# Block attention and a gated MLP on one core: the diagonal blocks of a pair's two heads transposed together

## The chip, the cores and the metric

The kernel runs on one core of a Trainium2 chip. The metric is the device time of one execution in microseconds. Before the change it is 771.0 us, the median of three runs (768.85, 771.0 and 771.5 us).

## What is computed

Eight batches of 576 rows. First an attention of 8 heads with 64 columns each, in which a row sees the keys of its own 64-row block and of all blocks before it; the heads' outputs stand side by side as 512 columns. Then a gated MLP whose gate mixes rows.

```python
scores = (1.0 / np.sqrt(D)) * np.matmul(q, k.transpose(0, 1, 3, 2))     # 8 x 8 x 576 x 576
scores = np.where(block_i >= block_j, scores, -1e9)                      # blocks of 64
attn = np.exp(scores - scores.max(-1, keepdims=True))
attn = attn / (attn.sum(-1, keepdims=True) + 1e-09)
x = heads_side_by_side(np.matmul(attn, v))                               # 8 x 576 x 512
h = gelu_tanh(x @ w_in)                                                  # 1024 columns
u, v = h[..., :512], h[..., 512:]
v_s = np.einsum('ts,bsd->btd', w_sg, layernorm(v) * g_ln) + b_sg[None, :, None]
return x + (u * v_s) @ w_out
```

## The kernel before

**Pairs.** Attention goes by pairs of heads, 32 in all, four to a batch. The two heads (a = 0, 1) lie on partitions 0 to 63 and 64 to 127 of the loaded q and k. `Scores` (L315) computes a pair's scores in float32 precision from split halves, for five query tiles i = 0 to 4 of 64, 128, 128, 128 and 128 rows. Tile i sees `EXT[i]` = 64 + 128 i keys, so its last 64 keys are its diagonal block: only its lower 64 rows see them (for i = 0, all of its 64). `maximum` (L349) takes the scores out of PSUM on VectorE (DVE) into `prob[a][i]`, with mask and running maximum; `exponent` (L364) makes probabilities of them in place on ScalarE (ACT), with their sums. Tile 4 has more keys than a PSUM bank has room for, so `FIRST` (L388) cuts it in two halves of 288 keys, put together with tiles 1 and 0.

**Values.** `Values` (L405) multiplies by v. TensorE (PE) needs the keys on partitions, so `turn` (L415) transposes 128x128 blocks of `prob` through PSUM banks pA, pB and pC, and a copy by ACT or DVE (`TE`, L398) takes each bank to a tile pt. `PLACES` (L399) says which block lands where: per head four blocks in A, five in B, five in C. The diagonal tile of i has only 64 keys; it is filled up with zeros to 128 (the zero fill is done once, L162 to L172) and transposed whole, of which 64 columns are used. `turn_sums` (L436) transposes tile 0 of each head, and the inverse sums spread over 64 columns (`rx`, five transposes), into banks pd and pe; ACT copies them to `rb`. `products` (L462) then runs 30 products, v as weights (128 keys by 64 columns), heads alternating, into bank ob and a corner of pe; `normalise` (L477) multiplies by the inverse sums and stores the tile to DRAM (`spill`).

**Loads.** All DMAs are issued in order from SyncE's queue (SP). `load_v` (L126) loads v of a pair as one DMA of 128 x 4 x 128 and one of 64 x 128 into one of two buffers; `load_qk` (L104) loads q and k two pairs ahead, GpSimd (POOL) splits them.

**The MLP as filler.** When a batch's four pairs are done, its MLP is cut into chunks (`v_part`, `u_part`, `s_part`, `o_part`). `slot` (L760), used for pairs 4 to 31, puts chunks (`hole`) between a pair's transposes, the next pair's scores and the products. `opening_slot` (L721), used for pairs 0 to 3, has no chunks to put there; meanwhile the weights of the MLP are loaded and split by ACT, DVE and POOL (`load_weight`, L212), until pair 8. PE's instructions stay in the order in which the code is written. Those of DVE, ACT and POOL do so for pairs 0 to 3; later a scheduler orders them, as it does the queue of SP throughout.

Of the kernel before, what the change touches and what calls it, by code (L numbers as in the profile page):

```python
# [9 lines left out]
F32 = mybir.dt.float32  # L10
# [10 lines left out]
def kernel(  # L21
# [12 lines left out]
    nc = tc.nc  # L34
# [54 lines left out]
    def turn(out, in_):  # L89
        return tensor.transpose(out, in_, ident)  # L90
# [34 lines left out]

    def load_v(n):  # L126
        b, h = PAIRS[n]
        v_f = v_bufs[n % 2]
        cols = slice(h * D, (h + 2) * D)
        nc.sync.dma_start(  # L130
            v_f[:, : NT - 1, :],
            v[b, : (NT - 1) * P, cols].rearrange("(j p) d -> p j d", p=P),
        )
        nc.sync.dma_start(v_f[:TAIL, NT - 1, :], v[b, S - TAIL :, cols])
        vals[n] = v_f

    load_qk(0)


    ident = cp.tile([P, P], F32, name="ident")  # L140
    make_identity(nc, ident)
    def warm(t, k):
        for _ in range(k):
# [12 lines left out]


    for s in (0, 1):
        t = cp.tile([P, NT, 2 * D], F32, name=f"v_f{s}")
        gpsimd.memset(t[TAIL:, NT - 1, :], 0.0)  # L160
        v_bufs.append(t)
    prob = []  # L162
    for s in (0, 1):
        row = []
        for i in range(NT):
            t = cp.tile([P, P * (i + 1)], F32, name=f"prob{s}_{i}")
            if i:
                gpsimd.memset(t[:, EXT[i] :], 0.0)
            else:
                gpsimd.memset(t, 0.0)  # L170
            row.append(t)
        prob.append(row)  # L172


    wi_h = cp.tile([P, NC, DFF], F32R, name="wi_h")
# [139 lines left out]
    class Scores:  # L315
# [33 lines left out]
        def maximum(self, a, i, lo, hi):  # L349

            r, e = slice(0, QN[i]), EXT[i]
            m = self.negm[a][r, i : i + 1]
            behind["V"] = vector.tensor_tensor_reduce(
                prob[a][i][r, lo:hi],
                self.where[a, i, lo],
                mask[r, MW - (hi - lo) :] if 0 < i and hi == e else mask[r, : hi - lo],
                -0.125,
                3.0e38 if lo == 0 else m,
                op0=ALU.add,
                op1=ALU.min,  # L360
                accum_out=m,
            )
# [36 lines left out]
    PLACES = {  # L399
# [3 lines left out]
    }  # L403

    class Values:  # L405
# [6 lines left out]
            self.sm = sc.sm  # L412
            self.pt = {}

        def turn(self, a, which):  # L415

            t = bank("p" + which)
            for i, j, c in PLACES[which]:
                turn(t[:, c : c + P], prob[a][i][:, P * j : P * (j + 1)])
            pt = sp.tile([P, 512], F32, tag="pt", name="pt" + which, bufs=6)  # L420
            copy(TE[a, which], pt, t)
            for i, j, c in PLACES[which]:
                self.pt[a, i, j] = pt[:, c + BLK : c + P] if i == j else pt[:, c : c + P]

        def inverse(self):

# [8 lines left out]

        def turn_sums(self):  # L436

            def spread(i):
                return self.rx[:, i, :]
# [4 lines left out]
            for i in (0, 1, 2):  # L444
                c = 2 * BLK + (i and BLK + P * (i - 1))
                turn(t[:, c : c + P], spread(i))
            for i in (3, 4):
                turn(t2[:, P * (i - 3) : P * (i - 2)], spread(i))
            w = 2 * BLK + EXT[2]
            d = sp.tile([P, 2 * BLK + S], F32, tag="rb", name="rb", bufs=1)  # L450
            copy("a", d[:, :w], t[:, :w])
            copy("a", d[:, w:], t2[:, : 2 * P])
            for a in (0, 1):
                self.pt[a, 0, 0] = d[:, a * BLK : (a + 1) * BLK]
            self.rb = d[:, 2 * BLK :]
            self.o0 = t2[:, 2 * P : 2 * P + BLK]

        def products(self):

            self.ob = bank("ob")  # L460
            for i in (4, 3, 2, 1, 0):
                for j in range(i + 1):  # L462
                    c = BLK if i == j and i else 0
                    w = BLK if i == j else P
                    c += P * (i - 1)
                    for a in (0, 1):
                        r = slice(a * D, (a + 1) * D)
                        dst = self.ob[r, c : c + w] if i else self.o0[r, :]
                        mm(
                            dst,  # L470
                            self.v[:, j, r],
                            self.pt[a, i, j],
                            start=j == 0,
                            stop=j == i,
                        )

        def normalise(self):  # L477

# [51 lines left out]
    def v_part(b, vv, vn, vn_t, u, g_s):  # L530
        need("v")
        x_s = xs[b]
        for st in range(NT):
            rows = P if st < NT - 1 else TAIL
            ss = slice(st * P, (st + 1) * P)
            acc = accumulator("accv")
            terms = []
            for c in range(NC):
                hi, lo, both = x_s[c]
                if st < NT - 1:  # L540
                    terms += [(hi[:, ss], wi_h, c), (lo[:, ss], wi_h, c), (hi[:, ss], wi_l, c)]
                else:
                    terms += [(both, wi_h, c), (both, wi_l, c)]
            for y, (l, w, c) in enumerate(terms):
                mm(acc, l, w[:, c, DH:], start=(y == 0), stop=(y == len(terms) - 1))
            x = vv[st] = page(F32, DH, "vv")[:rows, :]
            if st < NT - 1:
                last = scalar.copy(x, acc).ins
            else:
                vt = sp.tile([P, DH], F32, tag="pt", name="vt", bufs=6)  # L550
# [169 lines left out]

    def opening_slot(n, va):  # L721

        va.turn(0, "A")
        va.turn(1, "A")
        va.turn(0, "B")
        va.turn(1, "B")
        va.inverse()
        split_pending()
        va.turn(0, "C")
        va.turn(1, "C")  # L730
        load_v(n + 1)
        load_qk(n + 2)
        nx = Scores(n + 1)
# [26 lines left out]
    def slot(n, va):  # L760
# [4 lines left out]
            load_v(n + 1)  # L765
        if n + 2 < N:
            load_qk(n + 2)
        va.turn(0, "A")
        va.turn(1, "A")
        hole(g[0])  # L770
        run_side(k)
        split_pending()
        load_share(n, 0)
        va.turn(0, "B")
        va.turn(1, "B")
        hole(g[1])
        run_side(k)
        va.turn(0, "C")
        va.turn(1, "C")
        va.turn_sums()  # L780
        hole(g[2])
        run_gelu()
# [94 lines left out]
```

## Time and profile before

| | |
|---|---|
| median of three runs | 771.0 us |
| the profiled execution | 770.48 us, of which 768.7 us are the span of the profile |
| DVE, ACT, POOL busy | 483.5, 438.3, 299.2 us |
| mean granted TensorE clock | 0.993 of full speed |
| DMA | 65.84 MB, 86 GB/s on average; queue q1 takes 27.0% of the sixteen engines' span |

The profile is of one execution. An engine's busy time is the union of its instructions' records. PE means matmuls and transposes, PEld the loads of their stationary operand, which run beside them. A matmul's record overlaps the next one's, so the number of them in a stretch of time tells more than the length of one. Almost every row carries line 60, because all engine calls pass through one helper there: groups are told apart by their tiles. A row reads out<-in, and in a row of a timeline the bracket at its end is the idle time before it and what ended that. In the profile, a transpose of a block of `prob` is a matmul with `prob` as weights and the identity streaming through.

### The profile page before, as it was taken

The numbers are of one execution on the slowest core, as the hardware profiler recorded it, in microseconds if no ns is written. First come the engines' busy times: TensorE is split into PE (matmuls) and PEld (weight loads), VectorE is DVE, ScalarE is ACT, GpSimd is POOL, SyncE is SP. The second block draws the span as 40 slices with busy tenths as digits, with TensorE's granted clock in tenths as the row PEclk, the third lists the DMA queues.
The fourth block names the chain that finished last, engine by engine and source line by source line (L and its number), as shares of the span: only waits on it lengthen the run. The fifth ranks groups of instructions, "written<-read, shape, count | busy, mean of one in ns | idle before, by whom it ended". The sixth has DMA issues, their size and how long they took to land.

```text
span 768.7 us, 18262 instructions
## 1 busy us (share of the span) xinstructions
PE 751.7 (98%) x7106; PEld 711.2 (93%) x7106; DVE 483.5 (63%) x1477; ACT 438.3 (57%) x1096; POOL 299.2 (39%) x382
## 2 busy tenths in 40 slices
PE   8779998999999999999999999999999999999998
PEld 8778997989999899999999899998999989998998
DVE  6898789775945468544776348663495644942632
ACT  6666868558734767337754377544874467731600
POOL 3666695544234333243434234341234522322121
PEclk9989999999999999999999999999999999999999
DMA  8235233224232213312242112511124211120032
GB/s 261 82 103 178 64 107 92 77 90 133 85 119 62 63 64 109 94 47 63 64 140 78 33 61 76 172 48 48 49 91 141 63 42 53 53 88 17 1 124 93
DMA packets 46922, 65.84 MB, mean 86 GB/s; under 512 B 4082, under 2 KB 22514, under 8 KB 46836
## 3 DMA queue, kind: packets, MB, share of 16 engines
q1 hardware_dynamic: 46836, 64.67, 27.0%
q8 instruction: 56, 0.92, 0.5%
q14 instruction: 30, 0.25, 0.1%
HBM read 45.78 MB, written 18.87 MB: 84 GB/s over the span
## 4 chain that ended last, share of the span: by engine, by line
PE 92%; DVE 6%; ACT 1%; issue 1%; DMA 0%; POOL 0%; SPq 0%; DVEq 0%; ACTq 0%; POOLq 0%
PE accs L60 15%; PE accv L60 14%; PE acco L60 13%; PE accu L60 12%; PE s L60 10%; PE ob L60 10%; PE pB L60 5%; PE pC L60 5%; PE pA L60 3%; PE pd L60 2%; DVE w L60 2%; DVE prob L60 2%; PE pe L60 1%; ACT prob L60 1%; DVE vv L566 1%
## 5 line engine op out<-in xcount | busy, mean ns | idle before, releaser
L60 ACT ACTIVATE prob<-prob,negm 128x576 f32<-128x576 f32 (+3 forms) x320 | 176.4, 553 | 72.2 <-DVE negm L60 69.4
L60 DVE CUSTOM_DVE_ANT_0 prob<-s,mask 128x288 f32<-128x288 f32 (+3 forms) x320 | 121.5, 424 | 47.7 <-PE s L60 47.0
L60 POOL TENSOR_TENSOR xh<-x,xh 128x64 fp32r<-128x64 f32 x32 | 10.4, 325 | 205.5 <-DVE xh L60 145.4
L60 POOL TENSOR_TENSOR gl<-u,gh 128x288 fp32r<-128x288 f32 x64 | 51.8, 813 | 95.7 <-DVE gh L60 95.5
L60 PE MATMUL accu<-xh,wi_h 128*128 128x288 f32 x256 | 78.4, 306 | 0.0
L60 PE MATMUL accs<-ws_h,vh 128*128 128x288 f32 x256 | 77.9, 304 | 0.0
L60 PE MATMUL acco<-gh,wo_h 128*128 128x288 f32 x256 | 77.6, 303 | 0.0
L60 PE MATMUL accs<-ws_h,vl 128*128 128x288 f32 x256 | 75.6, 295 | 1.3 <-DVE vl L60 1.3
L60 PE MATMUL acco<-gl,wo_h 128*128 128x288 f32 x256 | 75.5, 295 | 0.0
L60 PE MATMUL accu<-xl,wi_h 128*128 128x288 f32 x256 | 75.5, 295 | 0.0
L60 PE MATMUL accs<-ws_l,vh 128*128 128x288 f32 x256 | 75.5, 295 | 0.0
L60 PE MATMUL accu<-xh,wi_l 128*128 128x288 f32 x256 | 75.4, 295 | 0.0
L60 PE MATMUL acco<-gh,wo_l 128*128 128x288 f32 x256 | 75.3, 294 | 0.0
L60 PE MATMUL accv<-wi_h,xh 128*128 128x512 f32 x160 | 65.3, 408 | 0.0
L60 DVE TENSOR_TENSOR u<-accs,u 128x288 f32<-128x288 f32 x64 | 29.1, 455 | 54.4 <-PE accs L60 53.9
L60 PE MATMUL accv<-wi_l,xh 128*128 128x512 f32 x160 | 63.0, 393 | 0.0
L60 PE MATMUL s<-kh,qh 64*128 64x288 f32 (+4 forms) x384 | 62.6, 322 | 0.0
L60 ACT ACTIVATION_READ_ACCUMULATOR prob<-prob,negm 128x1 f32 x320 | 59.9, 187 | 0.0
L60 PE MATMUL s<-kh,ql 64*128 64x288 f32 (+4 forms) x384 | 58.4, 301 | 0.0
L60 PE MATMUL s<-kl,qh 64*128 64x288 f32 (+4 forms) x384 | 57.3, 299 | 0.0
L60 ACT COPY vv<-accv 128x512 f32<-128x512 f32 x32 | 18.6, 581 | 67.1 <-PE accv L60 67.1
L60 PE MATMUL pB<-ident,prob 128*128 128x128 f32 x320 | 43.6, 283 | 8.5 <-DVE negm L60 6.8
(113 smaller groups left out, 2108.5 us busy)
## 6 DMA issues: line engine op xcount, KB each, us to landing
q_f<-in_qT SPq DMA_DIRECT2D x32, 288.0 KB, 3.6
k_f<-in_kT SPq DMA_DIRECT2D x32, 288.0 KB, 2.8
spill<-x SPq DMA_DIRECT2D x32, 288.0 KB, 2.9
xr<-spill SPq DMA_DIRECT2D x32, 288.0 KB, 2.9
out_T<-xr SPq DMA_DIRECT2D x32, 288.0 KB, 2.1
v_f<-in_v SPq DMA_DIRECT2D x32, 256.0 KB, 3.2
w<-in_w_in SPq DMA_DIRECT2D x16, 256.0 KB, 4.8
xr<-in_w_out SPq DMA_DIRECT2D x8, 256.0 KB, 2.7
```

Of the source, the lines that this page charges most:

```text
L60: return lambda *a, **k: pin(method(*a, **k), self.letter)
L566: tc.keep_in_program_order(nc.vector.scalar_tensor_tensor(x, x, stats[:rows, st, 0:1], g_bc[:rows, :], op0=ALU.subtract, op1=ALU.mult))
```

## The change

Both heads' probabilities of a query tile now lie in one tile of 2 x `EXT[i]` columns. The second head's keys stand there in falling order of their 64-key blocks, so that its diagonal block comes first and lies beside the first head's, which is last: columns 128 i to 128 i + 128 hold both. One transpose turns the two, with keys of head 0 on partitions 0 to 63 and of head 1 on 64 to 127. For i > 0 the lower 64 rows are wanted, so these go through a shifted identity (`turned`), which puts them first; the next transpose overwrites the other half. The five go to pd with the first two of the spread sums; the other three sums go to pe.

The remaining blocks off the diagonal are 20 for a pair, in five banks A0, A1, B0, B1 and C. DVE writes the second head's scores block by block in falling order, and tile 4 is cut at key 256, a whole number of blocks. The values follow: `v_f` has the halves of each 128-key group swapped for head 1, and a second tile `v_d` holds the diagonal blocks' values, head 0 on the upper and head 1 on the lower 64 partitions, with zeros beside them; so a diagonal product of one head still runs over 128 partitions. v now comes in seven DMAs with rows of 64 columns (256 bytes) where there were two with rows of 128 (512 bytes), and the diagonal blocks are read twice.

```diff
@@ load_v @@
+        v_f, v_d = vals[n] = v_bufs[n % 2]
+        lo, hi = slice(0, BLK), slice(BLK, P)
+        for a, r in ((0, lo), (1, hi)):
+            cols = slice((h + a) * D, (h + a + 1) * D)
+            x = v[b, : (NT - 1) * P, cols].rearrange("(j p) d -> p j d", p=P)
+            if a == 0:
+                nc.sync.dma_start(v_f[:, :, r], x)
+            else:
+                nc.sync.dma_start(v_f[lo, :, r], x[hi])
+                nc.sync.dma_start(v_f[hi, :, r], x[lo])
+            nc.sync.dma_start(v_d[r, : NT - 1, r], x[lo])
+            nc.sync.dma_start(v_d[r, NT - 1, r], v[b, S - TAIL :, cols])
@@ setup @@
+    turned = cp.tile([P, P + BLK], F32, name="ident")
+    ident = turned[:, :P]
+    gpsimd.tensor_copy(turned[:, P:], turned[:, :BLK])
+        t = cp.tile([P, NT - 1, 2 * D], F32, name=f"v_f{s}")
+        d = cp.tile([P, NT, 2 * D], F32, name=f"v_d{s}")
+    pairs = [cp.tile([P, 2 * EXT[i]], F32, name=f"prob{i}") for i in range(NT)]
+    prob = [[pairs[i][:, a * EXT[i] : (a + 1) * EXT[i]] for i in range(NT)] for a in (0, 1)]
@@ Scores @@
+            out = blocks(prob[a][i][r, :])
+            out = out[:, ::-1, :][:, lo // BLK : hi // BLK, :] if a else out[:, lo // BLK : hi // BLK, :]
-        FIRST = ((4, 0, SH), (1, 0, EXT[1])), ((4, SH, S), (0, 0, EXT[0]))
+        HALF = 256
+        FIRST = ((4, 0, HALF), (1, 0, EXT[1])), ((4, HALF, S), (0, 0, EXT[0]))
@@ Values @@
-    TE = {(0, "A"): "a", (1, "A"): "v", (0, "B"): "a", (1, "B"): "v", (0, "C"): "v", (1, "C"): "a"}
+    TE = {"A0": "a", "A1": "v", "B0": "a", "B1": "v", "C": "v"}
     PLACES = {
...
+        "A0": [(0, 4, j) for j in range(4)],
+        "A1": [(1, 4, j) for j in range(4)],
+        "B0": [(0, 3, 0), (0, 3, 1), (0, 3, 2), (0, 1, 0)],
+        "B1": [(1, 3, 0), (1, 3, 1), (1, 3, 2), (1, 1, 0)],
+        "C": [(0, 2, 0), (0, 2, 1), (1, 2, 0), (1, 2, 1)],
     }
@@ turn_sums @@
-            for a in (0, 1):
-                turn(t[:, a * BLK : a * BLK + P], prob[a][0])
+            for i in range(NT):
+                c = slice(i * BLK, i * BLK + P)
+                first = turned[:, BLK:] if i else ident
+                tensor.transpose(t[:, c], pairs[i][:, P * i : P * (i + 1)], first)
...
-            copy("a", d[:, :w], t[:, :w])
-            copy("a", d[:, w:], t2[:, : 2 * P])
+            copy("a", d[:, :512], t)
+            copy("a", d[:, 512:], t2[:, : 3 * P])
+            self.dg = [d[:, i * BLK : (i + 1) * BLK] for i in range(NT)]
@@ products @@
+                        if j < i:
+                            x, y = v_f[:, j, r], self.pt[a, i, j]
+                            dst = self.ob[r, P * (i - 1) : P * i]
+                        else:
+                            x, y = v_d[:, i, r], self.dg[i]
```

The tiles pt have five buffers where they had six, as a pair fills five. In what follows a name's number tells tiles apart: `prob_113` is the new tile of i = 3 for both heads, `prob_4_113` was head 0's of i = 4.

On PE, the first pair's transposes stood in this order before (pA, pB and pC, then after the next pair's scores pd and pe):

```order
L60 MATMUL pB<-ident,prob_4_113 128x128
L60 MATMUL pB<-ident,prob_3_111 128x128 x4
L60 MATMUL pB<-ident,prob_4_123 128x128
L60 MATMUL pB<-ident,prob_3_121 128x128 x4
L60 MATMUL pC<-ident,prob_1_107 128x128 x2
L60 MATMUL pC<-ident,prob_2_109 128x128 x3
L60 MATMUL pC<-ident,prob_1_117 128x128 x2
L60 MATMUL pC<-ident,prob_2_119 128x128 x3
```

and stand in this order now:

```order
L60 MATMUL pB_252<-ident,prob_113 128x128 x3
L60 MATMUL pB_252<-ident,prob_111 128x128
L60 MATMUL pB_259<-ident,prob_113 128x128 x3
L60 MATMUL pB_259<-ident,prob_111 128x128
L60 MATMUL pC<-ident,prob_112 128x128 x4
```

The diagonal blocks of i = 1 to 4 are gone from pB and pC; those of i = 1 moved ahead, from pC to pB, as far as they are off the diagonal. They come back in turn_sums, in this piece of PE's difference, which follows the scores of the next pair:

```order
-L60 MATMUL pd<-ident,prob_0_105 128x128
-L60 MATMUL pd<-ident,prob_0_115 128x128
-L60 MATMUL pd<-ident,rx 128x128 x3
-L60 MATMUL pe<-ident,rx 128x128 x2
+L60 MATMUL pd<-ident,prob_110 128x128
+L60 MATMUL pd<-ident,prob_111 128x128
+L60 MATMUL pd<-ident,prob_112 128x128
+L60 MATMUL pd<-ident,prob_113 128x128
+L60 MATMUL pd<-ident,prob_114 128x128
+L60 MATMUL pd<-ident,rx 128x128 x2
+L60 MATMUL pe<-ident,rx 128x128 x3
```

On DVE, the first maxima of the second pair (negm is the negated maximum, read out by a row of its own) stood like this before; a bracket names the engines whose semaphores an instruction waits for:

```order
L60 COPY ptC<-pC 128x512 [waits PE_49]
L60 ISA prob_4_113,negm<-s,mask 128x288 [waits PE_49]
L60 ISA negm 128x1
L60 ISA prob_1_107,negm<-s,mask 128x192
L60 ISA negm 128x1
L60 ISA prob_4_123,negm<-s,mask 128x288 [waits PE_49]
L60 ISA negm 128x1
L60 ISA prob_1_117,negm<-s,mask 128x192
L60 ISA negm 128x1
L60 ISA prob_4_113,negm<-s,mask,negm 128x288 [waits DVE_49,PE_49]
```

and now:

```order
L60 COPY ptC<-pC 128x512 [waits PE_49]
L60 ISA prob_114,negm<-s,mask 128x256 [waits PE_49]
L60 ISA negm 128x1
L60 ISA prob_111,negm<-s,mask 128x192 [waits PE_49]
L60 ISA negm 128x1
L60 ISA prob_114,negm<-s,mask 128x4x64
L60 ISA negm 128x1
L60 ISA prob_111,negm<-s,mask 128x3x64
L60 ISA negm 128x1
L60 ISA prob_114,negm<-s,mask,negm 128x320 [waits DVE_49,PE_49]
```

The maximum of tile 1 has a wait of its own now: it overwrites columns that the second transpose of pd reads. The second head's maxima are written in blocks of 64 (4x64, 3x64).

On SP's queue, the third time that a buffer of v is filled anew, before (spill is the normalised tile on its way to DRAM):

```order
L134 DMA v_f_101<-in_v 64x128 [waits DMAHW7_49,PE_49]
L130 DMA v_f_101<-in_v 128x4x128 [waits PE_49]
L108 DMA q_f<-in_qT 128x576 [waits DMAHW4_49,DMAHW1_49,Pool_49]
L483 DMA spill<-x 128x576 [waits DMAHW2_49,DVE_49]
L109 DMA k_f<-in_kT 128x576 [waits DMAHW6_49,DMAHW3_49,Pool_49]
```

and now:

```order
L139 DMA v_d_103<-in_v 64x64 [waits DMAHW3_49,PE_49]
L139 DMA v_d_103<-in_v 64x64 [waits DMAHW4_49,PE_49]
L134 DMA v_f_102<-in_v 128x4x64 [waits DMAHW5_49,PE_49]
L138 DMA v_d_103<-in_v 64x4x64 [waits DMAHW6_49,PE_49]
L136 DMA v_f_102<-in_v 64x4x64 [waits DMAHW7_49]
L490 DMA spill<-x 128x576 [waits DMAHW0_49,DVE_49]
L137 DMA v_f_102<-in_v 64x4x64 [waits DMAHW1_49]
L138 DMA v_d_103<-in_v 64x4x64 [waits DMAHW2_49,PE_49]
L108 DMA q_f<-in_qT 128x576 [waits DMAHW3_49,Pool_49]
L109 DMA k_f<-in_kT 128x576 [waits DMAHW4_49,Pool_49]
```

v's pieces stand on both sides of the spill, and the load of q, which stood ahead of the spill, follows them all.

More of the change, by code (lines that the diff above doesn't have):

```diff
@@ L158 @@
     for s in (0, 1):
[L159 to L172, printed above, removed]
+        t = cp.tile([P, NT - 1, 2 * D], F32, name=f"v_f{s}")
+        d = cp.tile([P, NT, 2 * D], F32, name=f"v_d{s}")
+        for a in (0, 1):
+            r = slice(a * D, (a + 1) * D)
+            gpsimd.memset(d[r, :, (1 - a) * D : (2 - a) * D], 0.0)
+        v_bufs.append((t, d))
+    pairs = [cp.tile([P, 2 * EXT[i]], F32, name=f"prob{i}") for i in range(NT)]
+    prob = [[pairs[i][:, a * EXT[i] : (a + 1) * EXT[i]] for i in range(NT)] for a in (0, 1)]
+    gpsimd.memset(pairs[0][BLK:, :], 0.0)
     wi_h = cp.tile([P, NC, DFF], F32R, name="wi_h")
@@ L352, in maximum, with blocks @@
             m = self.negm[a][r, i : i + 1]
+            def blocks(x):
+                return x.rearrange("p (n c) -> p n c", c=BLK)
+            out = blocks(prob[a][i][r, :])
+            out = out[:, ::-1, :][:, lo // BLK : hi // BLK, :] if a else out[:, lo // BLK : hi // BLK, :]
             behind["V"] = vector.tensor_tensor_reduce(
-                prob[a][i][r, lo:hi],
-                self.where[a, i, lo],
-                mask[r, MW - (hi - lo) :] if 0 < i and hi == e else mask[r, : hi - lo],
+                out,
+                blocks(self.where[a, i, lo]),
+                blocks(mask[r, MW - (hi - lo) :] if 0 < i and hi == e else mask[r, : hi - lo]),
                 -0.125,
@@ L413, in __init__, with turn @@
             self.pt = {}
-        def turn(self, a, which):
+        def turn(self, which):
             t = bank("p" + which)
[L418 to L423, printed above, removed]
+            pt = sp.tile([P, 512], F32, tag="pt", name="pt" + which, bufs=5)
+            for c, (a, i, j) in enumerate(PLACES[which]):
+                c = slice(c * P, (c + 1) * P)
+                k = BLK + P * (i - 1 - j) if a else P * j
+                turn(t[:, c], prob[a][i][:, k : k + P])
+                self.pt[a, i, j] = pt[:, c]
+            copy(TE[which], pt, t)
         def inverse(self):
@@ new lines, in turn_sums @@
+            for i in (0, 1):
+                turn(t[:, W + i * BLK : W + i * BLK + P], self.rx[:, i, :])
+            for i in (2, 3, 4):
+                turn(t2[:, P * (i - 2) : P * (i - 1)], self.rx[:, i, :])
+            d = sp.tile([P, W + S], F32, tag="rb", name="rb", bufs=1)
+            copy("a", d[:, :512], t)
+            copy("a", d[:, 512:], t2[:, : 3 * P])
+            self.dg = [d[:, i * BLK : (i + 1) * BLK] for i in range(NT)]
+            self.rb = d[:, W:]
+            self.o0 = t2[:, 3 * P : 3 * P + BLK]
@@ L458, in products @@
         def products(self):
             self.ob = bank("ob")
+            v_f, v_d = self.v
             for i in (4, 3, 2, 1, 0):
                 for j in range(i + 1):
-                    c = BLK if i == j and i else 0
-                    w = BLK if i == j else P
-                    c += P * (i - 1)
                     for a in (0, 1):
                         r = slice(a * D, (a + 1) * D)
[L468 to L475, printed above, removed]
+                        if j < i:
[3 more added lines that the diff above has]
+                            x, y = v_d[:, i, r], self.dg[i]
+                            c = P * (i - 1) + BLK
+                            dst = self.ob[r, c : c + BLK] if i else self.o0[r, :]
+                        mm(dst, x, y, start=j == 0, stop=j == i)
@@ L767, in slot @@
             load_qk(n + 2)
-        va.turn(0, "A")
-        va.turn(1, "A")
+        va.turn("A0")
+        va.turn("A1")
         hole(g[0])
```

43 lines of the change are left out of this document (10 added, 33 removed), and 3 rows, old and new, of the table PLACES.

## The prediction

> **What bounds the kernel now.** I read the busy shares first, then PE's waits, then stages of the span.
>
> ```profile
> PE 751.7 (98%) x7106; PEld 711.2 (93%) x7106; DVE 483.5 (63%) x1477; ACT 438.3 (57%) x1096; POOL 299.2 (39%) x382
> PE 92%; DVE 6%; ACT 1%; issue 1%; DMA 0%; POOL 0%; SPq 0%; DVEq 0%; ACTq 0%; POOLq 0%
> ```
>
> PE is busy for 98% of the span, and the chain that ended last is PE's own work for 92% of it. Busy matmuls overlap in the records, so the next question is whether PE ever stands still. These are rows of PE's waits (engine, tile, whom it waited for: us in total, times, longest), and of busy time by stage (each engine's busy us, then the granted clock, the DMA share and GB/s).
>
> ```profile
> PE pB L60 <- DVE negm L60: 6.8, 3, 3.5
> PE pA L60 <- ACT vh L60: 1.8, 1, 1.8
> PE accs L60 <- DVE vl L60: 1.3, 1, 1.3
> 40.00:55.00 15.00, 12.31 (x133) 11.02 (x133) 13.58 (x43) 10.12 (x31) 9.43 (x13) 0.88 0.29 85
> 90.00:110.00 20.00, 20.00 (x213) 19.50 (x212) 16.17 (x50) 16.70 (x42) 19.66 (x25) 1.00 0.38 110
> 110.00:150.00 40.00, 36.84 (x387) 35.30 (x386) 35.70 (x95) 26.50 (x65) 23.54 (x27) 1.00 0.25 79
> 300.00:400.00 100.00, 100.00 (x960) 95.06 (x957) 59.97 (x195) 59.59 (x151) 37.42 (x45) 1.00 0.27 84
> ```
>
> There are three stages. In the opening (pairs 0 to 3) DVE is busy for 13.58 of 15 us and PE waits for it. While the weights are split (up to 150 us) PE waits twice, 1.8 and 1.3 us. After that PE never waits before its last matmul, at full clock: from 300 to 400 us it has 100.00 of 100 us, with DVE and ACT at 60%. In this last stage a matmul less is its time less, as long as nothing new becomes late.
>
> **The price of one transpose.** Weight loads run ahead of their matmuls at the same pace; one full pair shows that pace without overlap (start, us, engine, operation, count).
>
> ```profile
> 384.75 1.14 PEld L60 LDWEIGHTS pC<-ident,prob 128*128 128x128 f32 x10
> 385.86 0.25 PEld L60 LDWEIGHTS pd<-ident,prob 128*128 128x128 f32 x2
> 386.08 0.36 PEld L60 LDWEIGHTS pd<-ident,rx 128*128 128x128 f32 x3
> 386.41 0.25 PEld L60 LDWEIGHTS pe<-ident,rx 128*128 128x128 f32 x2
> 386.63 0.19 PEld L60 LDWEIGHTS acco<-gh,wo_h 128*128 128x128 f32 x1
> ```
>
> Ten take 385.86 - 384.75 = 1.11 us, the next seven 386.63 - 385.86 = 0.77 us: **0.111 us each**, not the 283 ns that one matmul's record lasts.
>
> **What goes.** The groups of transposes over all 32 pairs:
>
> ```profile
> L60 PE MATMUL pB<-ident,prob 128*128 128x128 f32 x320 | 43.6, 283 | 8.5 <-DVE negm L60 6.8 <-ACT prob L60 1.6
> L60 PE MATMUL pC<-ident,prob 128*128 128x128 f32 x320 | 42.7, 283 | 0.0
> L60 PE MATMUL pA<-ident,prob 128*128 128x128 f32 x256 | 33.7, 273 | 1.8 <-ACT vh L60 1.8
> L60 PE MATMUL pd<-ident,prob 128*128 128x128 f32 x64 | 12.4, 276 | 0.0
> ```
>
> A pair turns 10 + 10 + 8 + 2 = 30 blocks of probabilities, and five spread sums beside them. Now it turns 4 + 4 + 4 + 4 + 4 off the diagonal and five double blocks on it: 25. Five go, 5 x 0.111 = **0.555 us a pair**. Score and value products keep their number and their total columns (256 + 320 for 288 + 288; ten 64-column diagonal products as before, still over 128 rows). For the 28 pairs from n = 4 on: 28 x 0.555 = **15.5 us**.
>
> **The opening.** There DVE's order sets the pace; these rows are of its third slot, PE and DVE, and the last is DVE's wait for the scores from 21 to 66 us.
>
> ```profile
> 42.73 2.13 PE L60 MATMUL pC<-ident,prob 128*128 128x128 f32 x10
> 44.78 0.40 PE L60 MATMUL s<-kh,qh 64*128 64x288 f32 x2
> 46.36 0.44 PE L60 MATMUL pd<-ident,prob 128*128 128x128 f32 x2
> 45.79 0.46 DVE L60 CUSTOM_DVE_ANT_0 prob<-s,mask 128x288 f32<-128x288 f32 x1 [0.88 <-PE s L60]
> 46.17 0.35 DVE L60 CUSTOM_DVE_ANT_0 prob<-s,mask 128x192 f32<-128x192 f32 x1
> DVE prob L60 <- PE s L60: 2.7, 3, 1.2
> ```
>
> At the lower clock a transpose costs some 0.2 us here (2.13 / 10), and eight fewer stand ahead of the scores (pB 8 for 10, pC 4 for 10): scores up to 1.6 us earlier. Against that, the second maximum, which ran 1.39 us after the scores began (46.17 - 44.78), now waits for the second diagonal transpose, behind all scores: 46.36 - 44.78 = 1.58, plus two transposes at about 0.11 and a handover of some 0.2, so about 2.0 us: 0.6 us later. Queued behind it on DVE is the whole softmax of the next pair, and ACT's exponents wait for that. DVE can win only the idle time it has, 2.7 us over three slots; if the scores come no earlier (pC may wait for ACT's exponents instead), it loses 4 x 0.6 = 2.4 us. I take **1.0 us won**, nearer to the idle time measured, and keep -2.7 and +2.4.
>
> **The weights.** PE's wait in this stage, and whom the ACT group that it names waits for:
>
> ```profile
> 122.77 0.63 PE L60 MATMUL pA<-ident,prob 128*128 128x128 f32 x4 [1.83 <-ACT vh L60]
> L60 ACT ACTIVATE vh<-vv,rs 128x512 fp32r<-128x512 f32 x32 | 22.9, 721 | 10.2 <-DVE vn_t L60 6.1 <-POOL rs L60 3.7 <-DVE vl L60 0.2
> ```
>
> ACT stands behind DVE and POOL there, and POOL is 19.66 of 20 us busy from 90 to 110. If that chain doesn't move, the savings of the three pairs before it turn into a longer wait: 3 x 0.555 = 1.7 us at most, 0 at least. I take **1.0 us given back**.
>
> **What costs nothing, and its cover.** The diagonal blocks now leave PSUM in rb's first copy, and the 17th product matmul needs it, where only the last four did.
>
> ```profile
> 386.72 0.53 ACT L60 COPY rb<-pd 128x448 f32<-128x448 f32 x1
> 389.99 1.09 PE L60 MATMUL ob<-ptA,v_f 128*64 128x128 f32 x16
> 390.92 1.06 PE L60 MATMUL ob<-ptB,v_f 128*64 128x64 f32 x20
> ```
>
> The copy ends at 387.25 and the 17th product starts at 390.92: 3.7 us of cover, filled by a chunk of feed-forward and the scores. ACT loses a 512-column copy per pair and rb's grow by 192 columns; DVE keeps three copies.
>
> DVE's six maxima per pair for the second head write blocks of 64 in falling order, five of them more than one block. No row shows that pattern. The nearest are
>
> ```profile
> L60 DVE CUSTOM_DVE_ANT_0 prob<-s,mask 128x448 f32<-128x448 f32 x64 | 37.2, 617 | 0.1
> L60 DVE CUSTOM_DVE_ANT_0 prob<-s,mask 128x192 f32<-128x192 f32 x64 | 22.5, 352 | 0.0
> L60 DVE CUSTOM_DVE_ANT_0 prob<-s,mask 64x64 f32<-64x64 f32 x64 | 13.5, 211 | 0.0
> ```
>
> From these an element costs (617 - 352) / 256 = 1.04 ns and a start 211 - 66 = 145 ns. The pattern costs nothing at one end; at the other, each further block costs a start: 24 blocks in five wide instructions, 19 x 0.145 = 2.8 us a pair. A gain is excluded: the elements are the same. I take 0, as the walk is still element by element; outside the opening DVE's free 40% would cover the 2.8 us anyway, inside it they would count.
>
> The V loads go from two DMAs to seven.
>
> ```profile
> v_f<-in_v SPq DMA_DIRECT2D x32, 256.0 KB, 3.2
> L134 SPq DMA_DIRECT2D v_f<-in_v x32: 471/472/556, 2.1 to 645.4; - x32
> q1 hardware_dynamic: 46836, 64.67, 27.0%
> DVE xr L60 <- DMA xr<-spill: 8.6, 4, 3.5
> 263.44 1.03 PE L60 MATMUL pA<-ident,prob 128*128 128x128 f32 x8
> 285.92 1.03 PE L60 MATMUL pA<-ident,prob 128*128 128x128 f32 x8
> ```
>
> Five more issues of 0.47 us are 2.4 us of SP per pair, against 285.92 - 263.44 = 22.5 us from one pair's first transposes to the next one's. Packets grow from 576 to 1664 a pair (512 to 256 bytes), bytes from 288 to 416 KB; at the mean rate of this kernel (27.0% of 768.7 us x 16 for 46836 packets, 71 ns each) that is 1088 x 0.071 / 16 = 4.8 us of the sixteen engines, an upper estimate, since these packets are smaller. The engines stand at 27%, so at most at 48%. V is asked for a slot ahead; past it on SP stand q, k and the spilled tiles, 1 to 2.4 us later. DVE's waits for spilled tiles are four, with a longest of 3.5 us, and end beside a PE that has work.
>
> The Trainium skill ("DMA: Bandwidth & Descriptors", Specifications) speaks against this part: it puts line rate at 512 bytes and more, with a read-modify-write below. By it the new packets would run under the rate of the old ones. No run here shows 256-byte packets yet; the sum stays, because the load has a slot to land in, but it is why the V rival below gets more than a trace of a chance.
>
> **The sum**, from the profiled execution's 770.48 us (span 768.7 and 1.8 around it, 0.5 under the median of 771.0): 770.5 - 15.5 - 1.0 + 1.0 = **755.0 us**, 2% less.
>
> **Rivals.**
> - *Late diagonal copy, slower.* ACT brings rb's copy behind other work, and PE stands before the 17th product of each pair. It decides once ACT is later than now by the 3.7 us of cover; a further 1.0 us in each of 28 pairs gives 755 + 28 = 783 us. For it: ACT's queue is in order and gets gelu work. Against it: ACT is 57% busy and loses a copy just ahead of rb. Chance 0.05.
> - *V traffic.* Loads of q, k and spilled tiles land late and PE waits in the filling and some slots: about one issue backlog of 2.4 us twice, 755 + 4.8 = 760 us. For it: the page's rule, and SP's fixed order with V's pieces ahead of q and k. Against it: the slot of lead. Chance 0.11.
> - *Blocks dear on DVE.* 2.8 us a pair in the DVE-bound opening (four or five softmaxes) gives 755 + 11 to 14 = 766 to 769 us; at half that price, 761. Chance 0.05.
> - *No gain per transpose.* The five double blocks go through a shifted identity. If those cost two ordinary ones each, 25 + 5 = 30, the old count: about 770.5 us. Against it: weights and moving tile have the same shape and type. Chance 0.04.
> - *More.* The opening wins all its idle 2.7 us and the weights hide nothing: 770.5 - 15.5 - 2.7 = 752, down to 751 with the fourth slot. Chance 0.06.
>
> **Numbers.** The forecast keeps 0.69, with its own range 751 to 759 (-2.7 and +2.4 of the opening, 0 to 1.7 of the weights, and the runs' own spread). With "more" and most of the V rival, 751 to 760 holds 8 in 10. A measurement of this kernel can tell about 0.3%, 2.3 us, from no change. Faster: 0.69 + 0.06 + 0.11 and half of the DVE case, 0.89. Same: the rest of that and no gain per transpose, 0.06. Slower: 0.05.
>
> **What will show it.** Right: 160 fewer transposes at the same 0.11 us pace, pd's double blocks included; PE at 98% without new waits after 150 us; DVE's second maximum in the opening behind pd, at no later time in the slot than now. Wrong: PE rows that wait for rb or v_d; block-pattern maxima longer than 617 ns for 448 columns; weight loads of pd slower than 0.111 us; PE waiting for q or k halves, or a longer wait at 122 us that eats more than 1.7 us.

## The result, and the profile after

The changed kernel takes **758.62 us**, the median of four runs (756.03 to 760.09), against 770.57 us for four runs of the kernel before. The ratio is 0.9848, with a 95% interval of 0.9818 to 0.9878: faster, by 1.2 to 1.8%. The forecast was 755.0 us, with a range of 751 to 760. The profiled execution took 758.84 us, with a span of 757.0 us.

These are the changed kernel's busy times and the chain that ended last, then PE's waits (engine, tile, whom it waited for: us in total, times, longest).

```profile
PE 735.8 (97%) x6946; PEld 693.2 (92%) x6946; DVE 474.8 (63%) x1477; ACT 425.3 (56%) x1064; POOL 305.0 (40%) x376
PE 73%; DVE 8%; POOL 5%; DMA 5%; ACT 3%; issue 3%; SPq 2%; DVEq 0%; POOLq 0%; ACTq 0%
PE pB L60 <- ACT prob L60: 9.1, 4, 4.1
...
PE accs L60 <- DVE vl L60: 1.7, 1, 1.7
PE acco L60 <- ACT ptB L60: 1.4, 1, 1.4
PE pA L60 <- ACT vh L60: 1.1, 1, 1.1
PE s L60 <- POOL ql L60: 0.9, 1, 0.9
PE pd L60 <- ACT rx L60: 0.5, 1, 0.5
PE acco L60 <- DVE negm L60: 0.4, 2, 0.2
```

The 160 instructions that were to go are gone (6946 for 7106), and PE is busy for 15.9 us less (735.8 for 751.7), close to the 15.5 priced for 28 pairs. But the span fell by only 11.7 us. The rest became waiting: PE fell to 97% of the span, and its share of the last chain from 92% to 73%. Among the waits that have no row in the kernel before, the one for pB's copy by ACT is the largest.

Stages, changed kernel first (us, busy us of PE, PEld, DVE, ACT, POOL with their instructions, granted clock, DMA share, GB/s); the last row is the kernel before, in a stretch that was not shown yet.

```profile
40.00:55.00 15.00, 11.98 (x129) 10.66 (x128) 12.76 (x39) 8.72 (x28) 8.57 (x11) 0.84 0.28 74
90.00:110.00 20.00, 20.00 (x213) 19.49 (x212) 16.71 (x50) 15.66 (x40) 19.65 (x24) 1.00 0.43 114
110.00:150.00 40.00, 36.29 (x372) 34.24 (x371) 34.79 (x94) 25.65 (x64) 27.91 (x29) 1.00 0.30 86
150.00:216.00 66.00, 64.17 (x615) 59.89 (x614) 45.20 (x147) 45.30 (x111) 29.85 (x39) 1.00 0.36 108
300.00:400.00 100.00, 100.00 (x943) 95.37 (x942) 58.27 (x190) 56.46 (x140) 38.14 (x45) 1.00 0.32 91
```

```profile
150.00:216.00 66.00, 66.00 (x631) 61.96 (x630) 47.51 (x148) 46.72 (x114) 30.62 (x41) 1.00 0.34 106
```

From 300 to 400 us PE is as full as before. From 150 to 216 us it was full before (66.00 of 66) and now stands still for 1.8 us.

To see where the time went, I read from each trace's timeline when a pair's first transposes (`pA<-ident,prob`) start. Times are us from the span's start, and "V in 7" is an experiment explained below.

| pair | before | after | difference | V in 7 | diagonals early | w_out later |
|---|---|---|---|---|---|---|
| 1 | 21.32 | 21.46 | +0.14 | 21.52 | 20.84 | 21.19 |
| 2 | 37.35 | 33.90 | -3.45 | 33.37 | 33.51 | 33.38 |
| 3 | 51.44 | 50.14 | -1.30 | 47.94 | 47.44 | 49.63 |
| 4 | 65.38 | 64.49 | -0.89 | 62.11 | 62.78 | 63.99 |
| 8 | 148.56 | 147.05 | -1.51 | 145.98 | 145.50 | 146.40 |
| 12 | 240.78 | 239.59 | -1.19 | 238.20 | 238.44 | 236.43 |
| 30 | 654.80 | 643.79 | -11.01 | 652.22 | 642.65 | 640.64 |
| 31 | 677.28 | 666.19 | -11.09 | 674.69 | 665.05 | 663.04 |
| end of the span | 768.7 | 757.0 | -11.7 | 766.1 | 755.9 | 753.9 |

From pair 12 to pair 30 the change wins 9.82 us in 18 pairs, 0.546 each, where 0.555 was priced. What is missing lies before: from pair 4 to 8 it won 0.62 us where four pairs should give 2.22, and from 8 to 12 it lost 0.32 us, where they should give 2.22 again. The slot from 30 to 31 gave 0.08. Each column is one execution. The changed kernel and the six edited ones below that differ from it only behind the start of pair 0 have that start between 10.46 and 11.12 us: half a microsecond in a single start tells nothing, and the distance between two starts of one execution tells more.

### The profile page after: what moved, and what is told of

Read it like the earlier page. It is cut to its first block, busy times and chain, and to the rows that moved or that the text cites. A ratio compares the mean times of both kernels' runs of the same rounds, so it can differ in the third digit from the quotient of the medians.

```text
span 757.0 us, 18446 instructions
## 1 busy us (share of the span) xinstructions
PE 735.8 (97%) x6946; PEld 693.2 (92%) x6946; DVE 474.8 (63%) x1477; ACT 425.3 (56%) x1064; POOL 305.0 (40%) x376
## 4 chain that ended last, share of the span: by engine, by line
PE 73%; DVE 8%; POOL 5%; DMA 5%; ACT 3%; issue 3%; SPq 2%; DVEq 0%; POOLq 0%; ACTq 0%
PE accs L60 16%; PE acco L60 11%; PE accv L60 11%; PE accu L60 9%; PE s L60 8%; PE ob L60 8%; PE pB L60 3%; PE pA L60 2%; PE pd L60 2%; DVE w L60 2%; ACT prob L60 2%; DVE prob L60 2%; DMA xr<-in_w_out 1%; PE pC L60 1%; POOL rs L60 1%
## 5 line engine op out<-in xcount | busy, mean ns | idle before, releaser
L60 DVE CUSTOM_DVE_ANT_0 prob<-s,mask 128x256 f32<-128x256 f32 (+3 forms) x320 | 119.8, 418 | 44.9 <-PE s L60 41.6
L60 PE MATMUL s<-kh,qh 64*128 64x320 f32 (+4 forms) x384 | 64.2, 328 | 0.0
L60 PE MATMUL s<-kh,ql 64*128 64x320 f32 (+4 forms) x384 | 59.8, 305 | 0.9 <-POOL ql L60 0.9
L60 PE MATMUL s<-kl,qh 64*128 64x320 f32 (+4 forms) x384 | 58.8, 304 | 0.3 <-POOL kl L60 0.3
L60 PEld LDWEIGHTS acco<-gh,wo_h 128*128 128x128 f32 x256 | 48.1, 188 | 3.4 <-ACT ptB L60 1.8
```

The lines of the kernel that those rows point to most:

```text
L60: return lambda *a, **k: pin(method(*a, **k), self.letter)
```

## The experiments

Each ran beside the kernel before on the same chip. The ratio is to that kernel, with its 95% interval. The span is of the profiled execution, and two kernels had a single run.

| kernel | median us | ratio | span us |
|---|---|---|---|
| five more transposes | 777.68 | 1.0092 (1.0066 to 1.0117) | 777.2 |
| V not loaded from pair 4 on | 757.64 | 0.9831 (0.9806 to 0.9856) | 755.9 |
| V in five DMAs | 758.28 | 0.9843 (0.9805 to 0.9881) | 756.0 |
| before, V in seven and a spare tile | 803.95 | 1.0432 (1.0407 to 1.0458) | 801.2 |
| before, V in seven | 766.74 | 0.9948 (0.9931 to 0.9965) | 766.1 |
| q and k ahead of V | 758.25 | 0.9830 (0.9800 to 0.9860) | 757.2 |
| after, half of w_out | 756.07 | one run | 754.3 |
| before, half of w_out | 773.15 | one run | 771.3 |
| diagonals early | 756.24 | 0.9816 (0.9793 to 0.9839) | 755.9 |
| w_out later | 754.67 | 0.9797 (0.9773 to 0.9820) | 753.9 |
| both | 753.88 | 0.9775 (0.9744 to 0.9807) | 752.3 |
| both, V in five DMAs | 753.81 | 0.9793 (0.9761 to 0.9824) | 751.1 |

**Five more transposes.** This puts the price of a transpose to the test.

```diff
@@ turn_sums @@
+            for j in range(5):
+                turn(t2[:, : P], pairs[4][:, P * j : P * (j + 1)])
             for i in (2, 3, 4):
                 turn(t2[:, P * (i - 2) : P * (i - 1)], self.rx[:, i, :])
```

> The changed kernel with five more 128x128 transposes per pair, put into columns of pe that the sums' transposes then overwrite. If each transpose in a slot that PE fills costs 0.111 us (the prediction's price), 28 pairs x 5 x 0.111 = 15.5 us come back: 758.6 + 15.5 = 774 us, and from pair 12 on the slots are as long as in the kernel before. In the opening they cost nothing up to 4 x 5 x 0.2 = 4 us, so at most 778. If the gain came from the ACT copy that went and not from PE, the time stays at 758.6 within 1 us.

It took 19.1 us more than the changed kernel by the medians, 20.2 by the spans. Of these, 4.98 lie before pair 4, 1 us more than the most that was expected there. From pair 13 to 30 it needs 391.43 us, the kernel before 391.36, the changed kernel 382.09: (391.43 - 382.09) / 17 / 5 = **0.110 us for each transpose**. The rival theory, that ACT's shorter work brought the gain, falls: ACT's work here is the changed kernel's.

**V not loaded from pair 4 on.** My first suspicion for the lost 4 us was V's DMAs.

```diff
@@ load_v @@
         v_f, v_d = vals[n] = v_bufs[n % 2]
+        if n > 3:
+            return
```

> The changed kernel without the V loads of pairs 4 to 31 (they use the V of pairs 2 and 3, so the attention of later pairs is left out in part); all other instructions stand in the same order. Some 4 us were lost between the start of pair 4 and that of pair 11. If V's seven DMAs on SP, or their packets, delay the weights and the halves of q and k there, these come back: 754 to 756 us. If the loss lies in how DVE, ACT and POOL are ordered there, nothing comes back: 758.6 within 1 us, and the waits at 112, 121, 125 and 201 us stay.

By the spans 1.1 us came back, and by the starts of the pairs 1.21: 0.46 before pair 4 and 0.96 from pair 4 to 8, of which 0.21 went again later. Of the 0.46, 0.34 stood already at pair 0 and aren't V's. So V's loads cost about 1 us, in the weights' stage. From pair 8 to 12 this kernel needs 92.75 us, the changed kernel 92.54, and the wait of 1.4 us for pB's copy stands: that loss is not V's.

**V in five DMAs.** The same bytes in the same rows, with two issues fewer.

```diff
@@ load_v @@
-            nc.sync.dma_start(v_d[r, : NT - 1, r], x[lo])
-            nc.sync.dma_start(v_d[r, NT - 1, r], v[b, S - TAIL :, cols])
+            z = v[b, :, cols].rearrange("(n p) d -> p n d", p=BLK)
+            nc.sync.dma_start(v_d[r, :, r], z[:, ::2, :])
```

> The changed kernel with V loaded by five DMAs instead of seven (the last diagonal block comes with the other four), the same bytes and packets; the other engines' order is the same. If the issues on SP are the loss (five more than before, now three more), two fifths of 4 us come back: 757 us. If the packets are, or neither, 758.6 within 1 us.

The medians do not tell it from the changed kernel (758.28 and 758.62). In the profiled executions it is 1.0 us ahead, and all of that by pair 8. From pair 4 to 8 it needs 81.88 us, the changed kernel 82.56, and the kernel without V's loads 81.60: with the same rows of 256 bytes most of the loss of that stage is gone. So it hangs on the number of issues, or on the times that follow from them, and not on the rows alone. Its pair 2 starts at 38.10 us where the changed kernel's starts at 33.90, though PE, DVE, ACT and POOL have the same order; the next experiments show why.

**The kernel before with V in seven DMAs.** The reverse: V's new loading without the new transposes. A first version loaded the extra pieces into a tile that nobody reads.

```diff
@@ load_v, kernel before @@
+            nc.sync.dma_start(spare[r, :, :], x[lo, :3])
```

> The kernel before with V cut into seven DMAs of 64-column rows, 1536 packets a pair (an extra 96 KB go to a tile that nobody reads); PE, DVE, ACT and POOL have the same order as before. If V's seven DMAs cost the 4 us that the changed kernel lost, 774 to 775 us here, lost between pairs 4 and 11. If not, 770.5 within 1 us. If the opening's 3.4 us at pair 2 came from V standing ahead of q and k on SP, pair 2 starts some 3 us earlier than in the kernel before here as well; if they came from the fewer transposes, it starts at the old time.

It took 804 us, far past both expectations, and answers another question. As nothing frees or reads the spare tile, the scheduler moved its loads up, ahead of q, k and the real pieces of V. These are SP's rows in that kernel (start, us, operation, count), and the wait of PE that grew most.

```profile
34.31 7.91 SPq L139 DMA_DIRECT2D spare<-in_v  x6
42.32 2.00 SPq L140 DMA_DIRECT2D v_f<-in_v  x2
44.37 0.59 SPq L108 DMA_DIRECT2D q_f<-in_qT  x1
PE s L60 <- POOL kh L60: 20.7, 3, 8.2
```

So SP issues can cost a lot, if q stands behind a backlog of them: pair 5 starts 30.35 us late. In the changed kernel PE's longest wait for a half of q or k is 0.9 us. A second version binds each piece to the buffers of the old loads.

```diff
@@ load_v, kernel before @@
+            if a == 0:
+                nc.sync.dma_start(v_f[:, :2, r], x[:, :2])
+                nc.sync.dma_start(v_f[:, 2 : NT - 1, r], x[:, 2:])
+            else:
+                nc.sync.dma_start(v_f[lo, : NT - 1, r], x[lo])
+                nc.sync.dma_start(v_f[hi, :2, r], x[hi, :2])
+                nc.sync.dma_start(v_f[hi, 2 : NT - 1, r], x[hi, 2:])
+            nc.sync.dma_start(v_f[:TAIL, NT - 1, r], v[b, S - TAIL :, cols])
```

> The kernel before with V in seven DMAs of 64-column rows (1152 packets of 256 bytes a pair where there were 576 of 512), the same data in the same places, nothing loaded twice, and each piece bound to the same buffers as the old loads; PE, DVE, ACT and POOL keep the order of before. If V's cutting costs what the changed kernel got back when its V loads were left out (1.2 us of the profiled executions, nearly all of it before pair 5 starts), 771 to 772 us. If SP's issues ahead of q and k act as in the run with the spare tile, more: over 775 us. If V costs nothing, 770.5 within 0.7 us.

All three expectations missed: it is **faster** than the kernel before, by 0.35 to 0.69%, and the gain lies in the opening, 3.27 us at pair 4; from 4 to 8 it loses 0.69, from 8 to 12 nothing. The timeline of the second slot shows how. The first four rows are of the kernel before, the next three of the one with V in seven; POOL splits q and k of pair 2 while DVE works on the integer words of w.

```profile
19.62 1.51 DVE L60 TENSOR_SCALAR w<-w 128x256 uint32<-128x256 uint32 x1
21.17 0.77 DVE L60 SCALAR_TENSOR_TENSOR w<-w 128x256 uint32<-128x256 uint32 x1
18.58 0.84 POOL L60 CAST qh<-q_f 128x576 fp32r<-128x576 f32 x1 [5.06 <-PE s L60]
19.50 1.48 POOL L60 TENSOR_TENSOR ql<-q_f,qh 128x576 fp32r<-128x576 f32 x1
```

```profile
19.54 0.29 DVE L60 TENSOR_SCALAR w<-w 128x256 uint32<-128x256 uint32 x1
19.86 0.42 DVE L60 SCALAR_TENSOR_TENSOR w<-w 128x256 uint32<-128x256 uint32 x1
22.66 0.67 POOL L60 CAST qh<-q_f 128x576 fp32r<-128x576 f32 x1 [8.74 <-PE pA L60]
```

The same instruction of the same shape takes 0.29 us with POOL idle and 1.51 us beside POOL's subtraction. With V's pieces ahead of them on SP, q and k come 2 to 3 us later (q of pair 2 is issued at 14.67 instead of 11.41), POOL starts at 22.66 instead of 18.58, and DVE, which sets the pace here, is through with w by 22.43 us, where the kernel before needs until 25.35. That is some 3 of the 4.2 us by which this slot is shorter (from pair 1 to 2, 11.85 us for 16.03); in the kernel before DVE then waits another 1.23 us for scores. In the changed kernel POOL starts at 22.83 and the same rows take 0.29 and 0.43 us.

**q and k ahead of V.** The calls of `load_qk` were put ahead of `load_v`, at the start and in both kinds of slot.

```diff
@@ opening_slot, slot @@
-        load_v(n + 1)
         load_qk(n + 2)
+        load_v(n + 1)
```

> The changed kernel with q and k of a slot issued ahead of V; the order of PE, DVE, ACT and POOL is the same, only SP's differs. If SP's order costs part of the 1.2 us, 757.5 to 758.6 us, and the wait for POOL's ql at 112 us shrinks. In the opening: q and k of pair 2 come about 3 us earlier, so POOL works beside DVE's integer instructions on w again; if that slows these, pair 2 starts at 37 to 38 us as in the kernel before instead of 33.9, and pair 4 within 1 us of 64.5. If they are not slowed by POOL, pair 2 starts at 33.9 or earlier.

The premise failed: the scheduler still issued q of pair 2 late, at 16.18 us (15.21 in the changed kernel). So it says nothing of an earlier q, and the time is the changed kernel's. The case that was meant is V in five DMAs: q at 13.10, POOL from 21.14, the last integer instructions stretched (0.75 us for 0.29), and pair 2 late. Of those 4.2 us the stretch explains 1.9; 1.1 more are a longer wait of DVE for pd (1.43 us for 0.29). The rest comes behind that, where the granted clock is 0.56 from 30 to 35 us and was 1.00 in the changed kernel; no run takes this part apart.

**Half of w_out, in both kernels.** From pair 7 on, w_out comes in eight pieces, one after the other through DMA, ACT, DVE and POOL.

```diff
@@ weights, o_part @@
-            ("o", load_weight(w_out, slice(0, DM), wo_h, wo_l, "xr", 0)),
+            ("o", load_weight(w_out, slice(0, DM // 2), wo_h, wo_l, "xr", 0)),
...
+            ws = slice(mo % 2 * P, (mo % 2 + 1) * P)
...
-                        w[:, c, ms],
+                        w[:, c, ws],
```

> The changed kernel with only four of the eight pieces of w_out loaded and split (the other half of the output uses them too, so its values are left out); the other instructions keep their order. Against the same cut in the kernel before. Between the starts of pairs 9 and 11 the changed kernel lost 1.42 us on the kernel before, where 1.1 should have been gained. If the pieces of w_out between DVE's maxima cause this (the last ones push r, the statistics and POOL's rs back, and with them ACT's vh and the copy of pB that PE waits for at 201 us), the wait at 201 us goes, and pairs 9 to 11 gain 1.1 us on the cut kernel before. If the cause is the changed kernel's own order of ACT (vh ahead of that copy), the wait stays.

> The kernel before with only four of the eight pieces of w_out (half of the output's values are left out), the control of the changed kernel cut in the same way. It had no PE wait between 150 and 216 us, so both theories expect the starts of pairs 9 to 11 22.5 us apart here as in the kernel before.

From pair 8 to 12 the cut changed kernel needs 90.04 us, the cut kernel before 92.22: 2.18 us less, against the 2.22 of the price. Uncut they were 92.54 and 92.22. So the whole loss between pairs 8 and 12 comes with the last four pieces of w_out in the changed kernel. The wait for pB's copy is gone though ACT still has vh ahead of it: vh now starts at 195.06 us instead of 200.06. So ACT's order alone is not the cause. (The control itself lost 2.2 us between pairs 7 and 8 on the uncut kernel before; I did not follow that up.)

These rows of the uncut changed kernel are the chain, from DVE by POOL and ACT to PE.

```profile
183.27 0.29 DVE L60 TENSOR_SCALAR xr<-xr 128x256 uint32<-128x256 uint32 x1 [1.69 <-DMA xr<-in_w_out]
195.76 2.64 POOL L60 TENSOR_SCALAR rs<-stats 128x5 f32<-128x5 f32 x1 [0.43 <-DVE stats L60]
200.06 0.72 ACT L60 ACTIVATE vh<-vv,rs 128x512 fp32r<-128x512 f32 x1 [3.16 <-POOL rs L60]
200.69 0.57 ACT L60 COPY ptB<-pB 128x512 f32<-128x512 f32 x1
201.31 0.40 PE L60 MATMUL acco<-gh,wo_h 128*128 128x288 f32 x1 [1.38 <-ACT ptB L60]
```

DVE stands for 1.69 us between two of pair 11's maxima, for a piece of w_out that has not landed; behind it come the softmax, the statistics, POOL's rs (2.64 us here, 0.56 in the kernel below), ACT's vh, and pB's copy, which PE needs. The kernel before has the same order on POOL and ACT without the wait:

```profile
195.63 0.65 POOL L60 TENSOR_SCALAR rs<-stats 128x5 f32<-128x5 f32 x1 [0.68 <-DVE stats L60]
198.40 0.71 ACT L60 ACTIVATE vh<-vv,rs 128x512 fp32r<-128x512 f32 x1
199.01 0.57 ACT L60 COPY ptB<-pB 128x512 f32<-128x512 f32 x1
```

Two delays meet here. Counted from the start of pair 10 (191.71 us in the changed kernel, 193.70 in the kernel before), rs starts after 4.05 us for 1.93, and then it takes 2.0 us longer. Each is more than PE's 1.38 us of waiting. rs takes 2.64 us in each of the five kernels that have this wait, and 0.56 to 0.65 us in those that lose it, so the two were never apart. That the last pieces of w_out set the wait off is shown; how much of it each of the two delays brings is not.

**w_out later, diagonals early.** These two try to mend what the runs before had shown. The first asks for the pieces later; the second turns the diagonals of pairs 0 to 3 before pC and the next scores, so that DVE's second maximum needs not wait for them.

```diff
@@ WS @@
-        8: (0, 2, 0, 3),
+        8: (0, 1, 0, 2),
+        9: (0, 1, 0, 1),
@@ opening_slot, the other kernel @@
         split_pending()
+        va.turn_diagonals()
         va.turn("C")
```

> The changed kernel with the pieces of w_out asked for later: three instead of five in pair 8's slot, two in pair 9's. ACT then has the copy of pB ahead of vh. If the 2.5 us between pairs 9 and 11 come from ACT standing at vh for POOL's rs with pB's copy queued behind it, the wait of 1.4 us at 201 us goes and the time falls by 1 to 2.5 us, to 756 to 757.6. If the last pieces are then late for the products with w_out, PE waits for wo_h or wo_l at pair 10 instead and nothing is won.

> The changed kernel with the five double diagonal blocks of pairs 0 to 3 turned ahead of pC and of the next pair's scores (in the order 4, 3, 1, 0, 2) instead of behind all scores; in the later slots they stay where they were. The kernel before with V in seven DMAs starts pair 4 at 62.11 us, the changed one at 64.49: 2.4 us. If that is DVE's second maximum waiting for pd (2.9 us in four waits), these waits go and pair 4 starts at 62 to 63.5 us (the five transposes now stand ahead of the scores, 0.6 to 1 us a slot, partly in PE's own wait for ACT's exponents): 756.5 to 758 us. If the 2.4 us come from something else (ACT's exponents, V's traffic), pair 4 starts at 64.5 or, by the later scores, up to 3 us after it.

With w_out later the four pairs from 8 to 12 take 90.03 us, the full price; the median falls by 4.0 us, more than the 1 to 2.5 expected. In the trace 3.16 us are won at pair 12, but 0.65 of them stood already at pair 8, before the edit acts, so 2.5 are its own. ACT now has the copy first, rs is early, and PE is full again (its rows: POOL, ACT, then the stage):

```profile
192.97 0.56 POOL L60 TENSOR_SCALAR rs<-stats 128x5 f32<-128x5 f32 x1
195.14 0.59 ACT L60 COPY ptB<-pB 128x512 f32<-128x512 f32 x1
150.00:216.00 66.00, 66.00 (x636) 62.44 (x635) 48.52 (x150) 46.38 (x112) 28.35 (x38) 1.00 0.40 118
```

With the diagonals early, pair 4 starts at 62.78 us, 1.71 earlier (0.41 of it stood already at pair 0). The first row is DVE's wait for them in the changed kernel, the second its wait for the scores up to 66 us in this one, where no wait for pd is left:

```profile
DVE prob L60 <- PE pd L60: 2.9, 4, 1.3
DVE prob L60 <- PE s L60: 2.4, 4, 1.2
```

At the end 1.1 us of the 1.71 are left. The granted clock differs here too (from 40 to 45 us 0.52 in the changed kernel, 0.95 in this one), so the waits and the clock share the gain in parts that no run tells.

**Both, and both with V in five DMAs.**

> The changed kernel with both edits: diagonals turned ahead of pC in the opening, and the later pieces of w_out. They work in stages apart (before pair 4, and after pair 8). If their gains add, by the profiled executions 1.1 + 3.1 = 4.2 us less than the changed kernel, 754 to 755 us by its profiled 758.84. If the earlier start of pair 4 only makes the weights' stage wait longer, as part of it did alone (1.7 us at pair 4, 1.1 at the end), the second edit's share is all that is left: 755.5.

> The same with V in five DMAs instead of seven. Alone that gave 1.0 us by the profiled executions, most of it before pair 8, in the opening too. If it adds, 753 to 754 us. If the opening's gain is the same one that the earlier diagonals won already, the same time as without it within 0.5 us.

753.88 and 753.81 us: the first as expected if the gains add (its profiled execution took 754.1), the second not to be told from it, nor either from w_out later alone (754.67; the intervals overlap). By the spans they are 4.7 and 5.9 us under the changed kernel. PE's waits in "both" have neither the one for pB's copy nor those for vh and vl; others took their place:

```profile
PE pB L60 <- ACT prob L60: 7.1, 4, 2.9
...
PE pd L60 <- ACT rx L60: 1.7, 1, 1.7
PE s L60 <- POOL ql L60: 1.5, 1, 1.5
PE s L60 <- POOL kl L60: 1.0, 1, 1.0
```

All kernels that keep the change and the whole computation are faster than the kernel before, except the one with five transposes added. The medians of the last two are some 4.8 us under the changed kernel's; the ratio of "both" lies clear of the changed kernel's interval, that of the other touches it (0.9824 and 0.9818).

## Why the prediction was right, and where its terms were not

The time lies in the upper part of the range, and the term that carries the sum, the price of a transpose, is right. Some of it is luck: the opening came out as forecast for a reason that the prediction did not have. Two of its own signs of being right failed to appear. PE has a new wait after 150 us, and DVE's second maximum in the opening comes later in its slot than before (in the third slot 3.33 us after the scores began, for 1.39). One of its signs of being wrong did appear: PE waits 0.9 us for a half of q.

**The price of a transpose** held. The double blocks go at the same pace, shifted identity included (weight loads of the changed kernel: five from 380.53 to 381.07, 0.108 us each), and five more cost 0.110 each. The rival of no gain per transpose falls.

```profile
380.53 0.58 PEld L60 LDWEIGHTS pd<-ident,prob 128*128 128x128 f32 x5
381.07 0.25 PEld L60 LDWEIGHTS pd<-ident,rx 128*128 128x128 f32 x2
```

**28 pairs of it** did not hold. This is the step whose size was off most: "After that PE never waits" was read in the kernel before and taken to hold in the changed one for every pair after 150 us. The prediction named the condition ("as long as nothing new becomes late"), but put no price on its failing. Pairs 8 to 12 gave -0.32 for 2.22 us. There PE's full row had hidden a chain over DMA, DVE, POOL and ACT, which came late once the scheduler had placed w_out's pieces otherwise (the last but one is asked for at 176.39 instead of 171.57 us). The kernels with half of w_out and with w_out later show that it is this chain; why the scheduler placed the pieces so, and why rs takes longer there, stays open. It isn't the loads of V from pair 4 on, as without them the order of the other engines and the wait are the same. The slot from 30 to 31 lost 0.47 of its 0.55 us; PE's waits name one stop there (0.18 us, for a maximum of DVE), and no run tried it.

**The opening**: 1.0 us won was forecast, 0.89 measured, but for another reason: the agreement is luck. The loss came out at the far end of its range: the kernel before with V in seven starts pair 4 at 62.11, the changed one, which also loads the diagonals' values twice, at 64.49, 2.38 us later, where 4 x 0.6 = 2.4 had been given for the second maximum behind pd. Moving the diagonals ahead won 1.3 to 1.71 of these, and the granted clock has a part in that. The single terms were not that even: in the third slot the second maximum came 3.33 us after the scores began (about 2.0 forecast, read at a clock of 0.66 from 40 to 45 us; in the changed kernel it is 0.52), in the second slot it waited 0.29 us only, and the four waits make 2.9 us.

```profile
41.87 0.58 PE L60 MATMUL s<-kh,qh 64*128 64x256 f32 x2
45.20 0.36 DVE L60 CUSTOM_DVE_ANT_0 prob<-s,mask 128x192 f32<-128x192 f32 x1 [1.27 <-PE pd L60]
```

The gain that outweighs the loss, 3.27 us, isn't DVE's idle time filled by fewer transposes: V's seven issues alone make it, for the most part by keeping POOL away from DVE. The prediction had V's issues "1 to 2.4 us later" for q and k as a possible harm only.

**The weights' stage**: 1.0 us given back was forecast (0 to 1.7), 1.60 measured from pair 4 to 8. V's loads are 0.96 of it, as leaving them out showed. The wait at 121 us for vh shrank (1.1 for 1.8), but vl's grew to 1.7 and POOL's ql came with 0.9. So POOL and DVE hid part of the saving, as said, and V's loads took the greater part, which the sum had at nothing.

**What was costed at nothing.** rb's copy ends at 382.19 and the 17th product matmul (a product makes two, so it belongs to the ninth product) starts at 385.90, 3.7 us of cover as before; no PE row waits for rb or v_d, so the late-copy rival falls. The blocks in falling order cost nothing: the maxima's means over both heads are 618 and 353 ns where they were 617 and 352. The loads of V were not quite free:

```profile
L60 DVE CUSTOM_DVE_ANT_0 prob<-s,mask 128x448 f32<-128x448 f32 x64 | 37.2, 618 | 0.0
L60 DVE CUSTOM_DVE_ANT_0 prob<-s,mask 128x192 f32<-128x192 f32 x64 | 22.6, 353 | 2.9 <-PE pd L60 2.9
q1 hardware_dynamic: 84212, 68.88, 31.0%
381.60 0.59 ACT L60 COPY rb<-pd 128x512 f32<-128x512 f32 x1 [0.65 <-PE pd L60]
385.90 0.28 PE L60 MATMUL ob<-rb,v_d 128*64 128x64 f32 x4
```

The queue's share rose from 27.0 to 31.0%, not to 48: the 71 ns a packet were, as said, an upper estimate. Without V from pair 4 on it is 24.4% of 755.9 us with 34484 packets, so V's 49728 packets took (0.310 x 757.0 - 0.244 x 755.9) x 16 / 49728 = 16 ns each. With the rest of the queue's time taken as equal in the kernel before (27.0% of 768.7 us), its 19456 packets for V come out at about 25 ns. These two are estimates. That is 16 and 20 bytes a nanosecond and engine: the rule quoted from the Trainium skill ("DMA: Bandwidth & Descriptors", Specifications), line rate from 512 bytes on, agrees in direction, as 256-byte rows move at some three quarters of the old rate. By the run without V all of V's loads cost about 1 us, a fifth of the V rival's 4.8 us, and the run with five DMAs says that the rows alone aren't what costs it.

In sum: 15.5 - 1.6 (weights) - 2.5 (w_out) - 0.5 (slot 30 to 31) + 0.9 (opening) = 11.8, against 11.7 us by the spans. The forecast was 3.6 us low: 2.5 for the w_out chain, 0.6 for the weights' stage and 0.5 for the slot from 30 to 31.

## What to carry to other kernels

A saving on an engine that never waits is worth its full pace only where the next chain has slack. Before multiplying by the number of slots, look in each stage for the chain that would be late next, above all where one-time work (weights) still runs beside. When a change cuts a load into more pieces, ask what they push back on the queue and whom that keeps away from whom: here a later q helped. To tell such effects apart, put the new loads into the old kernel.

## What the runs showed of the hardware

DVE's integer instruction on 128x256 words took 0.29 us with POOL idle and 1.51 us beside a POOL subtraction that ran from 19.50 to 20.98; it ended at 21.13, 0.15 after it. The Trainium skill ("SBUF — State Buffer", Who interferes with whom) says that the two share a pair of ports as an exclusive lock, held for a whole instruction, and that DVE needs it when it works in a two-port mode or has two inputs in SBUF. These rows agree with a lock; no run shows the mode in which this instruction worked. No run tells why POOL's small rs took 2.64 us in one kernel and 0.56 in another, since DVE centred vv beside it in both.
